# A router's table writes in two runs, and an expert's row transposes one unit earlier

## The chip, the cores and the metric

The kernel runs on one core of a Trainium2 chip. The metric is the device time of one execution in microseconds (us). The core's engines run side by side and wait for each other through semaphores: PE (TensorE, matrix products), DVE (VectorE), ACT (ScalarE), POOL (GpSimd, which here issues the indirect transfers) and SP (SyncE, which issues the plain transfers).

## What is computed

Three layers follow each other: block attention over chunks of 64 tokens, a dense MLP, and a mixture of eight experts of which every token uses two.

```python
x = attention(q, k, v)                        # 2304 tokens x 512
h = x @ w_in;  x = (h * clip(h + 3, 0, 6) / 6) @ w_out          # d_ff 2048
noisy = x @ w_gate + log1p(exp(x @ w_noise)) * noise            # 2304 x 8
top2, top2_w = two largest of noisy per token, softmax of the two
for e in range(8):
    for k in range(2):
        mask = top2[:, k] == e
        out[mask] += top2_w[mask, k, None] * (np.maximum(x[mask] @ w1[e], 0) @ w2[e])
```

## The kernel before

The 2304 tokens are 18 tiles of 128, in five batches of 4, 3, 4, 4 and 3 tiles (`BT`). A batch goes through the dense MLP in 16 units of 128 hidden columns: `mlp_s1` (line 346) makes a unit's hidden values in a PSUM bank, ACT and DVE turn them into the operand `g` (lines 425, 426, 430, 438), and `mlp_o` (line 359) multiplies the unit before into the accumulators. Every product is three passes over high and low parts of the operands, so that a unit of four tiles has 12 matmuls of 512 columns in `mlp_s1` and 12 in `mlp_o`. `regular(b, side, A, B, Z)` writes out batch b's units by hand: the lists A, B, Z and `side` hold what else goes in at each unit. The function `between` fills A, B and Z with the attention of the next batch (scores at line 232, row maximum at 239, subtraction at 249) and with the gate of the batch before. The order of PE, DVE and ACT is the order of the code there; from batch 4 on SP's is, too.

The gate of batch b-1 ends in `gate_ps`. DVE works out, for each token and each of its two experts, a row of a table in DRAM (`slot`, line 623), and POOL writes one entry (token number and weight) for every token by indirect transfers (line 626), one transfer for each tile and each of the two choices: eight for a batch of four tiles. For the first group of four tiles (tokens 0 to 511) this stands at unit 15 of batch 1. Nobody reads the table before batch 4.

Then come the experts as a list of groups: expert 0 in two parts (groups 0 and 1), experts 1 to 6 (groups 2 to 7) and expert 7 in two parts. An expert has eight units u. `exp_h` makes the hidden values of up to 600 rows in two halves of 300 columns, which go to two PSUM banks in turn (line 346, 24 matmuls), ACT and DVE make `g` of each half (lines 716, 717), and `exp_ot` (lines 749, 751, 753) multiplies the unit before. The list `side` says what else goes in at the end of each unit, for the experts that come next:

- `exp_slots_q`: SP loads an expert's slots (line 639) and their transposed copy `tq` (lines 648, 650); `exp_index`: DVE makes row indices `iq` of it (line 658).
- `exp_gather_q`: POOL gathers a tile of 128 rows of x by four indirect transfers (line 663; three for the last tile of 96 rows) into one of three buffers.
- `exp_tr_q`: DVE transposes a gathered tile (line 475), ACT copies it to the high part of the expert's operand (line 675), DVE subtracts for the low part (line 676). The operand alternates between two tiles, `Xa` and `Xe`. The five tiles of an expert are numbered 0 to 4. A gather buffer is free again after line 475.
- `pump`: ACT and DVE split one unit of expert weights (lines 171, 172), and SP loads another (line 165).

In expert 1 (group 2) `exp_tr_q` stood at units 3 to 7 for tiles 0 to 4 of expert 2, whose own units come next:

```python
        elif gi == 2:
            for i in range(nxt_[3]):
                at(side, 3 + i, exp_tr_q, nxt_[0], i)
                if 0 < i < 3:
                    at(side, i, exp_index, nxt_[0], i, (2, nxt_[3])[i - 1])
                if i > 0:
                    at(side, i, exp_gather_q, nxt_[0], i)
```

Of the kernel before, what the change touches and what calls it, by code (L numbers as in the profile page):

```python
# [80 lines left out]
def tile_kernel(ctx, tc, qkv, w1u, w2u, wg, noise, out):  # L81
# [527 lines left out]
        nc.vector.tensor_tensor(offs2, early, base, op=ALU.subtract)  # L609
        nc.vector.scalar_tensor_tensor(offs2, offs2, 0.0, offs, op0=ALU.max, op1=ALU.add)  # L610

    def gate_ps(g):
        t0, nt = GRP[g]
        m12, m = st.pop(("m", g))
        lg = st.pop(("lg", g))
        pos = lg[:, :nt * NE].rearrange("p (t e) -> p t e", t=nt)
        of = offs2 if g == len(GRP) - 1 else offs
        qf = small([P, 5, NE], "qf")[:, :nt]
        nc.vector.tensor_tensor(qf, pos, of[:, None, :].to_broadcast([P, nt, NE]), op=ALU.add)
        nc.vector.tensor_tensor(m12, m12, qf[:, None].to_broadcast([P, 2, nt, NE]), op=ALU.mult)  # L620
        sf = small([P, 2, 5, 1], "sf")[:, :, :nt]
        nc.vector.tensor_reduce(sf, m12, axis=AX.X, op=ALU.add)
        nc.vector.tensor_copy(slot[:, t0:t0 + nt, :], sf.rearrange("p k t o -> p t (k o)"))  # L623
        for t in range(t0, t0 + nt):
            for k in range(2):
                s = nc.gpsimd.indirect_dma_start(  # L626
                    out=table, out_offset=bass.IndirectOffsetOnAxis(ap=slot[:, t, k:k + 1], axis=0),
                    in_=pay[:, t, k, :], in_offset=None)
                for o in st.setdefault("tab_st", []):
                    tc.declare_no_dep(s.ins, o.ins, reason="every slot is given once")  # L630
                st["tab_st"].append(s)
# [372 lines left out]
    def between(b, attn, gates, top, per):  # L1004


        A, B, Z, nt, n0 = {}, {}, {}, BT[b], st.get("tick", 0)
        before = BT[b - 1]

        def s2_(u, k, f, *a):  # L1010
            n = n0 + 3 + k if u == 0 else n0 + 3 + before + (3 + nt) * (u - 1) + 3 + k
            at(ticks, n, f, *a)

        def s1_(u, k, f, *a):
            n = n0 + k if u == 0 else n0 + 3 + before + (3 + nt) * (u - 1) + k
            at(ticks, n, f, *a)


        for i, u in enumerate(attn):
            t = B0[b + 1] + i  # L1020
            if nt > 3:
                s2_(u, nt, att_sc, t, 0, outer)
            else:
                s1_(u, 2, att_sc, t, 0, outer)
            at(B, u, att_mx, t, False)
            at(B, u, att_e, t)
            at(B, u + 1, att_n, t)
            if nt > 3:
                s1_(u + 2, 3, att_pt, t)
                at(A, u + 2, att_at, t, at_[0])  # L1030
                s2_(u + 2, nt, att_xo, t)
                end = (B, u + 2)
            else:
                s2_(u + 2, 1, att_pt, t)
                at(B, u + 2, att_at, t, at_[0])
                s1_(u + 3, 2, att_xo, t)
                end = (Z, u + 3)
            at(*end, att_hi, t)
            at(*end, att_lo, t)
            if t + 2 < NTILE:  # L1040
                at(*end, load_tile, t + 2, bufs[4 + t % 2])
        first = B0[b - 1]
        for u, n in gates:
            ts = list(range(first, first + n))
            first += n
            for i, t in enumerate(ts):
                at(B, u - n - 1 + i, gate_l, t)
                at(B, u - n + i, gate_d, t)
            if nt > 3:
                s2_(u, nt, gate_mm, ts, ENDS[0])  # L1050
                at(B, u, gate_lp, ts)
                s1_(u + 1, 2, gate_rt, ts, ENDS[1])
                s1_(u + 1, 2, gate_rr, ts)
            else:
                p5 = bank("p5", [P, DM], "lg")
                s1_(u + 1, 1, gate_mm, ts, p5)
                at(A, u + 1, gate_lp, ts)
                s1_(u + 2, 1, gate_rt, ts, p5[:, 2 * P:])
                s1_(u + 2, 1, gate_rr, ts)
        for i in range(4):  # L1060
            at(B, top + i // per, gate_top, b - 1, 1)
        pos, pm = ENDS[1] if nt > 3 else bank("p5", [P, DM], "pos"), top + 5 - per
        s2_(pm, 1, gate_pm, b - 1, pos)
        at(B, pm, gate_ps, b - 1)
        return A, B, Z


# [36 lines left out]
    with tc.manual_schedule(engines={nc.tensor.engine, nc.vector.engine, nc.scalar.engine}):  # L1104
        steps(REST)
        prev = [(0, U1 - 1)]
        regular(1, {}, *between(1, (1, 4, 7, 10), ((4, 2), (8, 2)), 12, 2))
        side = {}
        at(side, 10, zero_out)
        regular(2, side, *between(2, (1, 3, 5, 7), ((4, 2), (8, 1)), 10, 2))  # L1110
        side = {}
        for j in range(3):
            at(side, 12 + j, load_raw, U1 + j)
        regular(3, side, *between(3, (1, 3, 5), ((4, 2), (8, 2)), 10, 1))
# [13 lines left out]
    for gi, (key, e, r0, nt, off) in enumerate(groups):  # L1128
# [11 lines left out]
            at(side, 5, exp_gather_q, after[0], 0)  # L1140
        elif gi == 2:
            for i in range(nxt_[3]):
                at(side, 3 + i, exp_tr_q, nxt_[0], i)
                if 0 < i < 3:
                    at(side, i, exp_index, nxt_[0], i, (2, nxt_[3])[i - 1])
                if i > 0:
# [117 lines left out]
```

## Time and profile before

| | |
|---|---|
| runs of the kernel before | 911.08, 912.23, 912.97 us; median 912.23 |
| the profiled execution | 911.34 us |
| its span, first to last instruction | 909.6 us |
| mean granted TensorE clock | 0.996 |
| PE busy | 892.3 us (98% of the span) |
| DVE, ACT, POOL busy | 495.4, 320.6, 230.8 us |
| chain of work that ended last | PE 88%, DVE 5%, DMA 2%, ACT 2%, POOL 1% |

The 1.74 us between the span and the time of the same execution lie outside the first and the last instruction. Of the 17.3 us of the span in which PE is not busy, most is at its start and end. A matmul's end in the profile is modelled, so a stretch of PE is best compared with an equal stretch of the same number and shape of matmuls.

### The profile page before, as it was taken

The page shows a single profiled execution, that of the slowest core. Times are in us where ns is not written, and L with a number is a line of the kernel's source. Part 1 is how long each engine was busy: PE and PEld are TensorE (multiplying, and loading weights), DVE is VectorE, ACT ScalarE, POOL GpSimd, SP SyncE. Part 2 cuts the span into 40 slices and gives each one's busy share as a digit, 9 for nine tenths or more (in the row PEclk, how much of TensorE's full clock was granted, in tenths as well). Part 3 has the DMA queues.
Part 4 walks back from the last instruction along what each step waited for, and adds up shares of the span by engine and source line. Part 5 has one row for each costly group of instructions (what it writes and reads, how often), then busy time and mean ns, then how long its engine had stood idle before and what let it go on. Part 6 is the DMA issues. An engine that isn't in the chain of part 4 may idle for free.

```text
span 909.6 us, 15438 instructions
## 1 busy us (share of the span) xinstructions
PE 892.3 (98%) x6295; PEld 794.0 (87%) x6295; DVE 495.4 (54%) x953; ACT 320.6 (35%) x610; POOL 230.8 (25%) x212
## 2 busy tenths in 40 slices
PE   8999999999999999999999999999999999999995
PEld 5777788887878877888888899999999999999995
DVE  7999955545552553447552544555656555562421
ACT  5555433332332332244551432333333333331110
POOL 0000000030002000023103465455383634606051
PEclk9999999999999999999999999999999999999998
DMA  9745522123228410025541762386786857655462
GB/s 343 251 127 177 172 70 94 36 70 71 71 102 304 129 46 1 1 70 118 157 144 37 171 148 76 92 222 145 200 173 149 188 146 208 151 156 78 111 84 31
DMA packets 68930, 116.39 MB, mean 128 GB/s; under 512 B 17872, under 2 KB 38480, under 8 KB 68848
## 3 DMA queue, kind: packets, MB, share of 16 engines
q1 hardware_dynamic: 57552, 95.33, 35.2%
q0 software_dynamic: 11296, 19.97, 12.4%
q8 instruction: 51, 0.84, 0.4%
q14 instruction: 31, 0.25, 0.1%
HBM read 85.13 MB, written 30.09 MB: 127 GB/s over the span
## 4 chain that ended last, share of the span: by engine, by line
PE 88%; DVE 5%; DMA 2%; ACT 2%; POOL 1%; issue 1%; another core or an unknown queue 1%; SPq 0%; POOLq 0%; ACTq 0%; DVEq 0%
PE bp L346 38%; PE bp L359 21%; PE bp L749 10%; PE bp L753 7%; PE bp L419 4%; PE bp L392 3%; PE pair L314 1%; PE pair L232 1%; POOL table L626 1%; PE pair L293 1%; DMA lead<-in_qkv_dram 1%; DMA table<-pay,slot 1%; DVE u L204 1%; PE bp L690 1%
## 5 line engine op out<-in xcount | busy, mean ns | idle before, releaser
L359 PE MATMUL bp<-w,g 128*128 128x512 f32 (+3 forms) x921 | 230.4, 393 | 0.5 <-ACT g L430 0.4
L359 PEld LDWEIGHTS bp<-w,g 128*128 128x128 f32 (+2 forms) x921 | 166.6, 186 | 35.5 <-DVE g L438 0.9
L346 PE MATMUL bp<-Xa,w 128*128 128x300 f32 (+3 forms) x1152 | 193.7, 319 | 0.5 <-issue 0.3
L346 PEld LDWEIGHTS bp<-Xa,w 128*128 128x128 f32 x1152 | 172.2, 188 | 11.7 <-issue 1.6
L749 PE MATMUL bp<-g,w 128*128 128x352 f32 x576 | 161.4, 323 | 0.0
L753 PE MATMUL bp<-g,w 128*128 128x248 f32 x564 | 155.2, 277 | 0.0
L626 POOL DMA_INDIRECT table<-pay,slot x36 | 36.6, 1015 | 436.7 <-DVE slot L623 427.3
L663 POOL DMA_INDIRECT xrq<-x2d,iq x114 | 117.4, 1030 | 103.7 <-DVE arena L475 62.0
L717 DVE SCALAR_TENSOR_TENSOR g<-bp,g 128x300 fp32r<-128x300 f32 (+2 forms) x127 | 59.2, 470 | 155.1 <-ACT g L716 108.3
L716 ACT ACTIVATE g<-bp 128x300 fp32r<-128x300 f32 (+2 forms) x127 | 53.2, 422 | 224.0 <-PE bp L346 181.2
L749 PEld LDWEIGHTS bp<-g,w 128*128 128x128 f32 x576 | 108.2, 188 | 0.1
L753 PEld LDWEIGHTS bp<-g,w 128*128 128x128 f32 x564 | 106.1, 188 | 0.5
L346 PE MATMUL bp<-Xb,w 128*128 128x384 f32 (+2 forms) x480 | 104.2, 360 | 0.0
L346 PE MATMUL bp<-Xe,w 128*128 128x300 f32 (+1 forms) x672 | 99.8, 303 | 0.0
L346 PEld LDWEIGHTS bp<-Xe,w 128*128 128x128 f32 x672 | 95.5, 188 | 0.8
L346 PEld LDWEIGHTS bp<-Xb,w 128*128 128x128 f32 x480 | 84.7, 188 | 11.3 <-issue 1.1
L172 DVE TENSOR_TENSOR w<-raw,w 128x1024 fp32r<-128x1024 f32 x64 | 78.2, 1222 | 29.2 <-ACT w L171 23.1
L807 POOL DMA_INDIRECT out_dram<-arena,tab x40 | 65.1, 1628 | 104.9 <-ACT arena L787 43.4
L426 DVE SCALAR_TENSOR_TENSOR r<-r,bp 128x384 f32<-128x384 f32 (+1 forms) x64 | 39.7, 620 | 82.5 <-ACT r L425 76.7
L425 ACT ACTIVATE r<-bp,b 128x384 f32<-128x384 f32 (+1 forms) x64 | 40.4, 632 | 106.9 <-PE bp L346 102.6
L171 ACT ACTIVATE w<-raw 128x1024 fp32r<-128x1024 f32 x64 | 67.1, 1049 | 4.7 <-PE bp L359 4.5
L438 DVE TENSOR_TENSOR g<-r,g 128x384 fp32r<-128x384 f32 (+1 forms) x64 | 40.1, 626 | 40.7 <-ACT g L430 39.4
(178 smaller groups left out, 796.9 us busy)
## 6 DMA issues: line engine op xcount, KB each, us to landing
raw<-in_w2u_dram SPq DMA_DIRECT2D x64, 512.0 KB
raw<-in_w1u_dram SPq DMA_DIRECT2D x24, 512.0 KB
arena<-in_qkv_dram SPq DMA_DIRECT2D x14, 768.0 KB
turned<-arena SPq DMA_DIRECT2D x24, 304.0 KB
out_dram<-zero SPq DMA_DIRECT2D x4, 1536.0 KB
yr<-turned SPq DMA_DIRECT2D x6, 1024.0 KB
rawx<-in_w1u_dram SPq DMA_DIRECT2D x8, 512.0 KB
x2d<-x SPq DMA_DIRECT2D x15, 256.0 KB
```

Source lines behind the costliest of these rows:

```text
L171: nc.scalar.activation(w[:, 0], raw, AF.Copy)
L172: nc.vector.tensor_tensor(w[:, 1], raw, w[:, 0].bitcast(F32), op=ALU.subtract)
L346: nc.tensor.matmul(dst, w[:, a, kd * P:(kd + 1) * P], x[:, b, kd, t0:t0 + n], start=(k == 0), stop=(k == 3 * KD - 1))
L359: nc.tensor.matmul(y[:gi.shape[2]], gi[:, a], w[:, b, DM + c:DM + c + y.shape[1]], start=(first and j == 0), stop=(last and j == 2))
L425: nc.scalar.activation(r, st["h", b], AF.Relu, bias=b3)
L626: s = nc.gpsimd.indirect_dma_start(out=table, out_offset=bass.IndirectOffsetOnAxis(ap=slot[:, t, k:k + 1], axis=0), in_=pay[:, t, k, :], i ...
L663: nc.gpsimd.indirect_dma_start(out=xr[:, c * P:(c + 1) * P], out_offset=None, in_=x2q, in_offset=bass.IndirectOffsetOnAxis(ap=st["iq", key ...
L716: nc.scalar.activation(hi[:, t0:t0 + n], h, AF.Relu)
L717: nc.vector.scalar_tensor_tensor(lo[:, t0:t0 + n], h, 0.0, hi[:, t0:t0 + n].bitcast(F32), op0=ALU.max, op1=ALU.subtract)
L749: nc.tensor.matmul(acc[c][:, :BIG], wc, g[a][:, :BIG], start=first, stop=last)
L753: nc.tensor.matmul(small[:, off:off + CAP - BIG], wc, g[a][:, BIG:CAP], start=False, stop=last and off > 0)
L807: s = nc.gpsimd.indirect_dma_start(out=out, out_offset=bass.IndirectOffsetOnAxis(ap=tab[:n, i, 0:1], axis=0), in_=y, in_offset=None, compu ...
```

## The change

`gate_ps` no longer converts all slots of a group and writes all entries. It keeps the slot numbers and calls the new `gate_sc(g, i0, i1)`, which converts those of tiles i0 to i1 and writes their entries. For the first group it is called for tiles 0 and 1 where all four stood, and for tiles 2 and 3 from the side list of batch 2 at unit 1. All other groups are converted and written in one piece as before. In expert 1 the row transposes of expert 2 are written at units 2 to 6 in place of 3 to 7.

```diff
-    def gate_ps(g):
+    def gate_ps(g, n=None):
...
         nc.vector.tensor_reduce(sf, m12, axis=AX.X, op=ALU.add)
-        nc.vector.tensor_copy(slot[:, t0:t0 + nt, :], sf.rearrange("p k t o -> p t (k o)"))
-        for t in range(t0, t0 + nt):
+        st["sf", g] = sf
+        gate_sc(g, 0, n or nt)
+
+    def gate_sc(g, i0, i1):
+        t0 = GRP[g][0]
+        nc.vector.tensor_copy(slot[:, t0 + i0:t0 + i1, :], st["sf", g][:, :, i0:i1].rearrange("p k t o -> p t (k o)"))
+        for t in range(t0 + i0, t0 + i1):
             for k in range(2):
                 s = nc.gpsimd.indirect_dma_start(
...
-        at(B, pm, gate_ps, b - 1)
+        at(B, pm, gate_ps, b - 1, None if b > 1 else 2)
...
         at(side, 10, zero_out)
+        at(side, 1, gate_sc, 0, 2, BT[0])
         regular(2, side, *between(2, (1, 3, 5, 7), ((4, 2), (8, 1)), 10, 2))
...
             for i in range(nxt_[3]):
-                at(side, 3 + i, exp_tr_q, nxt_[0], i)
+                at(side, 2 + i, exp_tr_q, nxt_[0], i)
```

DVE at the seam of batches 1 and 2, before: from the end of `gate_ps` (line 622) to unit 2 of batch 2. `r` and `g` are the MLP's operands, `x` the batch's output, `mx` and `arena` belong to the attention.

```order
L622 TENSOR_REDUCE sf<-m_1985 128x2x4
L623 CAST slot<-sf 128x8
L426 SCALAR_TENSOR_TENSOR r<-r,bp_466 128x512
L438 TENSOR_TENSOR g<-r,g 128x512
L460 TENSOR_SCALAR x_2102<-bp_465 128x512
L426 SCALAR_TENSOR_TENSOR r<-r,bp_467 128x512
L438 TENSOR_TENSOR g<-r,g 128x512
L239 TENSOR_REDUCE mx<-pair_72 128x8
L249 TENSOR_TENSOR arena<-pair_72,mx 128x512
L426 SCALAR_TENSOR_TENSOR r<-r,bp_466 128x512
```

And with the change (the conversion is now line 628):

```order
L622 TENSOR_REDUCE sf<-m_1985 128x2x4
L628 CAST slot<-sf 128x4
L426 SCALAR_TENSOR_TENSOR r<-r,bp_466 128x512
L438 TENSOR_TENSOR g<-r,g 128x512
L460 TENSOR_SCALAR x_2098<-bp_465 128x512
L426 SCALAR_TENSOR_TENSOR r<-r,bp_467 128x512
L438 TENSOR_TENSOR g<-r,g 128x512
L239 TENSOR_REDUCE mx<-pair_72 128x8
L249 TENSOR_TENSOR arena<-pair_72,mx 128x512
L628 CAST slot<-sf 128x4
L426 SCALAR_TENSOR_TENSOR r<-r,bp_466 128x512
```

The conversion of eight columns became two of four, the second seven DVE instructions later, behind the attention's subtraction.

DVE in the last two units of expert 1, before: `g` is the operand of the unit, `arena` and `Xa` the gathered tile of expert 2, `w` a weight unit, and line 706 opens expert 2.

```order
L717 SCALAR_TENSOR_TENSOR g<-bp_466,g 128x300
L717 SCALAR_TENSOR_TENSOR g<-bp_467,g 128x300
L475 STREAM_TRANSPOSE arena<-xrq 128x512
L676 TENSOR_TENSOR Xa<-arena,Xa 128x4x128
L172 TENSOR_TENSOR w<-raw,w 128x1024
L717 SCALAR_TENSOR_TENSOR g<-bp_466,g 128x300
L717 SCALAR_TENSOR_TENSOR g<-bp_467,g 128x300
L475 STREAM_TRANSPOSE arena<-xrq 128x384
L676 TENSOR_TENSOR Xa<-arena,Xa 128x4x96
L706 CAST g<-zeros 128x264
```

And with the change (lines 717, 676, 706 are now 722, 681, 711):

```order
L722 SCALAR_TENSOR_TENSOR g<-bp_466,g 128x300
L722 SCALAR_TENSOR_TENSOR g<-bp_467,g 128x300
L475 STREAM_TRANSPOSE arena<-xrq 128x384
L681 TENSOR_TENSOR Xa<-arena,Xa 128x4x96
L172 TENSOR_TENSOR w<-raw,w 128x1024
L722 SCALAR_TENSOR_TENSOR g<-bp_466,g 128x300
L722 SCALAR_TENSOR_TENSOR g<-bp_467,g 128x300
L711 CAST g<-zeros 128x264
```

The last tile's transpose and subtraction stand ahead of the last unit's two `g` instructions, no longer behind them. The instructions of PE, POOL and SP stand in the same order in both kernels; ACT's copies (line 675) move with the transposes.

## Rows read from the trace of the kernel before

**Rows 1.** The page, part 1: engine, busy us, share, instructions.

```profile
PE 892.3 (98%) x6295; PEld 794.0 (87%) x6295; DVE 495.4 (54%) x953; ACT 320.6 (35%) x610; POOL 230.8 (25%) x212
```

**Rows 2.** Waits of PE, whole span: us in total, times, longest us.

```profile
PE bp L346 <- issue: 0.3, 1, 0.3
PE bp L346 <- DVE Xa L676: 0.2, 1, 0.2
```

**Rows 3.** Timeline of PE, batch 2: start, us, line, tiles, count [idle before <-releaser].

```profile
204.29 0.69 PE L232 MATMUL pair<-arena 64*64 64x64 f32 x32
204.91 1.99 PE L346 MATMUL bp<-Xa,w 128*128 128x512 f32 x7
207.22 1.41 PE L346 MATMUL bp<-Xa,w 128*128 128x512 f32 x5 [0.32 <-issue]
...
218.52 3.03 PE L346 MATMUL bp<-Xa,w 128*128 128x512 f32 x12
```

**Rows 4.** Timeline of POOL: first and last of the first group's eight table writes.

```profile
195.89 1.16 POOL L626 DMA_INDIRECT table<-pay,slot  x1 [193.63 <-DVE slot L623]
...
205.03 0.97 POOL L626 DMA_INDIRECT table<-pay,slot  x1 [0.30 <-issue]
```

**Rows 5.** Timeline of DVE in the same stretch.

```profile
194.79 0.17 DVE L623 CAST slot<-sf 128x8 int32<-128x8 f32 x1
...
207.44 0.69 DVE L239 TENSOR_REDUCE mx<-pair 128x8 f32<-128x512 f32 x1 [2.96 <-remote]
```

**Rows 6.** Timeline of all engines, the row of SP in the same stretch.

```profile
203.69 3.64 SPq L483 DMA_DIRECT2D xq<-x2d  x8
```

**Rows 7.** Windows: stretch, us, PE, PEld, DVE, ACT, POOL busy (count), clock, DMA share, GB/s.

```profile
384.00:396.00 12.00, 12.00 (x59) 10.40 (x57) 3.66 (x6) 3.83 (x7) 7.76 (x8) 1.00 0.20 59
420.00:432.00 12.00, 12.00 (x62) 10.86 (x61) 7.77 (x12) 6.17 (x9) 8.72 (x8) 1.00 0.71 134
...
616.00:628.00 12.00, 12.00 (x90) 12.00 (x89) 6.04 (x9) 4.32 (x7) 9.56 (x9) 1.00 0.84 166
```

**Rows 8.** Timeline of PE: expert 1's last unit and expert 2's first.

```profile
570.28 3.47 PE L346 MATMUL bp<-Xe,w 128*128 128x300 f32 x24
...
576.99 1.98 PE L346 MATMUL bp<-Xa,w 128*128 128x300 f32 x13
579.15 1.78 PE L346 MATMUL bp<-Xa,w 128*128 128x300 f32 x11 [0.19 <-DVE Xa L676]
```

**Rows 9.** Timeline of ACT in expert 1's last unit.

```profile
575.88 0.73 ACT L716 ACTIVATE g<-bp 128x300 fp32r<-128x300 f32 x2 [5.17 <-remote]
```

**Rows 10.** Timeline of DVE at the same seam.

```profile
576.34 0.85 DVE L717 SCALAR_TENSOR_TENSOR g<-bp,g 128x300 fp32r<-128x300 f32 x2 [4.37 <-ACT g L716]
577.10 0.85 DVE L475 STREAM_TRANSPOSE arena<-xrq 128x384 f32<-128x384 f32 x1
578.54 0.56 DVE L676 TENSOR_TENSOR Xa<-arena,Xa 128x384 fp32r<-128x384 f32 x1 [0.59 <-ACT Xa L675]
```

**Rows 11.** Timeline of POOL: first and last of eight gathers for expert 3, and the next.

```profile
564.42 0.95 POOL L663 DMA_INDIRECT xrq<-x2d,iq  x1 [4.81 <-DVE iq L658]
...
573.18 0.95 POOL L663 DMA_INDIRECT xrq<-x2d,iq  x1 [0.30 <-issue]
578.22 0.95 POOL L663 DMA_INDIRECT xrq<-x2d,iq  x1 [4.10 <-DVE arena L475]
```

**Rows 12.** Timeline of DVE: unit 2 of expert 1, up to unit 3's first half.

```profile
541.60 0.22 DVE L658 TENSOR_SCALAR iq<-tq,quarter 128x12 int32<-128x12 int32 x1
542.16 1.23 DVE L172 TENSOR_TENSOR w<-raw,w 128x1024 fp32r<-128x1024 f32 x1 [0.34 <-ACT w L171]
546.17 0.47 DVE L717 SCALAR_TENSOR_TENSOR g<-bp,g 128x300 fp32r<-128x300 f32 x1 [2.78 <-ACT g L716]
```

**Rows 13.** Chain that ended last: start, us, what; one gather's way to its landing.

```profile
441.52 3.94 DMA xr<-x2d,tab
```

## The prediction

> **What bounds the kernel now.** The first thing to read is the share of each engine: PE is busy for 892.3 of 909.6 us, 98%, and the next engine, DVE, for 54% [rows 1]. So a change can only take away places where PE stands still or matmuls that PE need not do. This change does not touch the matmuls. The second view is therefore the list of what PE waited for. Two entries of it lie where the change works, and each occurs once in the whole span: 0.3 us before line 346 with no releaser ("issue"), and 0.2 us before line 346 for the subtraction of line 676 [rows 2]. The third view, the timeline of PE, puts them at 207.22 us (unit 1 of batch 2) and at 579.15 us (expert 2's first unit) [rows 3, 8]. Whatever the change does to other engines, these two places are what it can give back.
>
> The wait that the list shows is less than what PE loses, because the matmuls just ahead of it come late as well. I compare equal blocks. Batch 2's unit 1 has its 12 matmuls of 512 columns from 204.91 to 207.22 + 1.41 = 208.63, 3.72 us; the same 12, also right behind a tile's scores, take 3.03 us at 218.52 [rows 3]. Loss: **0.69 us**. Expert 2's first 24 matmuls run from 576.99 to 579.15 + 1.78 = 580.93, 3.94 us; the 24 of the unit before take 3.47 us [rows 8]. Loss: **0.47 us**.
>
> **Part one, the table writes in two runs.** Before, POOL writes eight transfers in one run, from 195.89 to 205.03 + 0.97 = 206.00, one every (205.03 - 195.89) / 7 = 1.31 us [rows 4]. At the end of that run two things happen together. The scores' matmuls are over at 204.29 + 0.69 = 204.98 [rows 3], yet DVE's row maximum, which waits for nothing but them, starts at 207.44 after an idle time that the profile can only call "remote" [rows 5]: the signal from PE was some 2.5 us late. And PE itself issues its next matmuls 0.69 us late while it waits for nobody. I take both for one cause, a stretch in which signals are held up at the end of a long run of indirect transfers, because the same sign (a late "remote" signal) comes again at 575.88 [rows 9], 1.75 us behind the end of another run of eight, 573.18 + 0.95 = 574.13 [rows 11].
>
> With the change four writes run from 195.89 to about 195.89 + 3 x 1.31 + 0.97 = 200.8, over 3.5 us before the scores start. The second conversion stands on DVE behind the row maximum and the subtraction. If the signal is on time these run from about 205.0 to 206.4, the conversion (at most the 0.17 us of the wide one) to 206.6, and POOL starts 195.89 - 194.79 = 1.1 us after it [rows 4, 5], at about 207.7, and is done at about 212.6. The extra conversion costs nothing: DVE was idle for 2.96 us there [rows 5]; without that cover it would be 0.17 us. No further wait is added on PE, ACT or SP, and nobody reads the table before batch 4. So this part is worth -0.69 us if the run's length is the cause, 0 if it is not, and +0.69 us if the second run brings the same loss to its own end and the first keeps its own. I take -0.69: the loss stands at the end of the run and nowhere near it before. Against it speaks that two other runs of eight writes, from 384 and from 420 us, leave PE at 12.00 of 12.00 us [rows 7].
>
> **Part two, expert 2's transposes one unit earlier.** Before, the last tile's transpose, copy and subtraction come behind both `g` instructions of unit 7. ACT got the hidden values' signal at 575.88, after 5.17 us of idle time [rows 9], so the two `g` instructions ran until 576.34 + 0.85 = 577.19 and the tile from 577.10 to 578.54 + 0.56 = 579.10 [rows 10]; PE, already in expert 2, waited for exactly this. In the changed order the tile is done one unit of 576.99 - 570.28 = 6.7 us earlier [rows 8], ahead of the late signal. The 0.47 us go. What is late next is the PSUM bank: PE starts expert 2 at 576.99, and the first of the two `g` instructions that free its bank ends at about 576.34 + 0.47 = 576.81 (0.47 from rows 12). That leaves 0.18 us of margin.
>
> What the move costs elsewhere: one tile's three steps took 579.10 - 577.10 = 2.0 us for 96 rows [rows 10], so at most 2.7 us for 128. In unit 2, which gets a tile that it did not have, DVE is idle for 0.34 us and 2.78 us, 3.1 us together [rows 12]; it fits, with 0.4 us to spare. Behind it on DVE are queued the index of line 658 and the weight split of line 172, both up to 2.7 us later. The index releases POOL's gather of tile 2: issue at about 545, four transfers 1.25 us apart [rows 11], the last at about 549, landed by 553 if it takes the 3.94 us that a gather on the chain took [rows 13]. It is needed two units behind the index's old place, at 541.6 + 13.4 = 555. The split releases SP's weight load and the slot loads behind it, whose first reader is in unit 5, over 20 us on. Units 3 to 6 trade one tile for the next. Price 0; if the gather's cover went, DVE would wait at the transpose with `g` of the next unit behind it, but by less than the unit's own slack. This part: -0.47 us, bounds -0.47 to what the third rival below costs.
>
> **The sum.** -0.69 - 0.47 = -1.16 us, against the profiled execution's 911.34 us: 910.2. That execution lies 0.89 us below the median of the runs, 912.23; from the median the same difference gives **911.1 us**, -0.13%.
>
> **Rivals.** *First: the stall at 207 is not the run's doing.* SP issued eight transfers from 203.69 to 207.33 [rows 6], just where PE lost its time, and the change leaves these where they are. Together with the two other runs of eight that cost PE nothing [rows 7] this is a serious case. Only part two counts: 912.23 - 0.47 = 911.8. The Trainium skill speaks for this rival: "SBUF — State Buffer", section "Who interferes with whom", states that a DMA never contends with a compute engine and that PE never waits on anyone, and by that rule a run of transfers cannot hold PE, so the sum would be -0.47 rather than -1.16 us. The trace agrees at 384 and 420 us (12.00 of 12.00), not at 207, where PE lost 0.69 us.
>
> *Second: both losses belong to that one execution.* They come from late signals, and three runs of one kernel differ by 1.9 us. Then the change does what it says and nothing comes of it: 912.2.
>
> *Third, slower: the longer gather run.* Tile 4's transpose frees the buffer of expert 3's third tile a unit earlier. Before, POOL stopped for 4.10 us at that point [rows 11]; now it goes on behind the eighth gather, twelve in one run, until about 564.42 + 11 x 1.25 + 0.95 = 579.1. If signals stay late until 1.75 us after the run's end, ACT gets its signal at 580.9 in place of 575.88, the bank is free 0.93 us later, at 581.8, and PE stands from 576.99 on: 4.8 us. With part one's gain the time is 912.23 - 0.69 + 4.8 = 916.3. It decides at 0.18 us: any lateness beyond today's by more than this margin is paid in full. Against it: from 616 to 628 POOL issued nine transfers with hardly a break, 9.56 us busy, and PE was at 12.00 of 12.00 [rows 7].
>
> **How the numbers follow.** Forecast (both go) 0.50; first rival 0.27; second 0.10; third 0.08; unprofiled runs that hold more of such stalls than the profile, and so gain more than 1.16 us, 0.05. A measurement of this kernel tells about 0.2%, 1.8 us, from no change. Faster than that means under 910.4: the last case, and from the forecast and the first rival what the runs' scatter of about 0.9 us puts there, 0.15 together. Slower means over 914.0: the third rival and a remainder of scatter, 0.08. The rest, 0.77, is within 0.2%. The range of 910.0 to 912.9 holds the forecast and the first two rivals with that scatter, and leaves out most of the third.
>
> **What would show it.** Right: 12 matmuls of batch 2's unit 1 in about 3.03 us with no idle time, the row maximum starting near 205 in place of 207.44, two runs of four writes; in expert 2 the first 24 matmuls in about 3.47 us in one piece, the last transpose near 568 to 570. Wrong in part one: a block of 3.7 us again, there or at the second run's end. Wrong in part two: PE waiting at about 577 for line 717's successor, with ACT idle on a late signal behind a gather run of twelve. The prediction as a whole fails if PE's idle time moves by more than these two places, for which I see no cause in the order of instructions.

## The result, and the profile after

The changed kernel takes **920.56 us** (916.16 to 923.01, six runs) beside 912.17 us of the kernel before (911.08 to 912.97, six runs): a ratio of **1.0096**, interval 1.0081 to 1.0110. The forecast was 911.1 us with a range of 910.0 to 912.9; the time lies 7.7 us above its upper end. The profiled execution of after took 922.26 us, 10.92 us more than the one of before.

Page of after, part 1, and below it the waits of PE over the whole span (us in total, times, longest us); the answering rows of before are [rows 1, 2].

```profile
PE 898.8 (98%) x6295; PEld 799.5 (87%) x6295; DVE 494.8 (54%) x954; ACT 321.3 (35%) x610; POOL 231.0 (25%) x212
```

```profile
PE bp L346 <- issue: 1.9, 4, 1.1
...
PE bp L758 <- issue: 1.6, 2, 1.4
...
PE bp L754 <- issue: 1.4, 2, 1.0
```

PE is busy 6.5 us longer with the same 6,295 matmuls, so some of them ran slower, and it stood still for 4.9 us with no releaser, 0.3 us before. The other engines do what they did.

**Part one came out as forecast.** The same seam of batch 2 on PE, DVE and POOL, as in [rows 3 to 5] (columns: start, us, engine, line, operation, tiles, count, [idle before <-releaser]; L631, L628 and L239 of after are L626, L623 and L239 of before):

```profile
204.88 3.03 PE L346 MATMUL bp<-Xa,w 128*128 128x512 f32 x12
```

```profile
205.02 0.69 DVE L239 TENSOR_REDUCE mx<-pair 128x8 f32<-128x512 f32 x1 [0.60 <-PE pair L232]
...
206.35 0.16 DVE L628 CAST slot<-sf 128x4 int32<-128x4 f32 x1
```

```profile
199.89 0.97 POOL L631 DMA_INDIRECT table<-pay,slot  x1 [0.30 <-issue]
206.79 0.97 POOL L631 DMA_INDIRECT table<-pay,slot  x1 [5.93 <-DVE slot L628]
```

The twelve matmuls are in one piece of 3.03 us (3.72 before), and the row maximum starts at 205.02 with PE as its releaser, not at 207.44 as "remote".

**The loss stands in expert 1 and 2.** POOL's gathers, first and last of two runs in which one follows the other after 0.30 us:

```profile
543.52 1.42 POOL L668 DMA_INDIRECT xrq<-x2d,iq  x1 [4.38 <-issue]
...
556.62 0.94 POOL L668 DMA_INDIRECT xrq<-x2d,iq  x1 [0.30 <-issue]
567.85 0.94 POOL L668 DMA_INDIRECT xrq<-x2d,iq  x1 [10.29 <-DVE iq L663]
...
581.94 0.95 POOL L668 DMA_INDIRECT xrq<-x2d,iq  x1 [0.30 <-issue]
```

The first run has eleven gathers (tiles 2 to 4 of expert 2), the second twelve (tiles 0 to 2 of expert 3). PE in the same stretches:

```profile
555.64 0.87 PE L346 MATMUL bp<-Xe,w 128*128 128x300 f32 x4
556.77 0.30 PE L346 MATMUL bp<-Xe,w 128*128 128x300 f32 x1 [0.26 <-issue]
558.17 0.44 PE L346 MATMUL bp<-Xe,w 128*128 128x300 f32 x2 [1.10 <-issue]
...
559.59 4.36 PE L346 MATMUL bp<-Xe,w 128*128 128x300 f32 x16 [0.31 <-issue]
...
567.86 3.48 PE L346 MATMUL bp<-Xe,w 128*128 128x300 f32 x24
...
574.47 3.46 PE L346 MATMUL bp<-Xe,w 128*128 128x300 f32 x24
...
579.91 0.28 PE L758 MATMUL bp<-g,w 128*128 128x248 f32 x1 [0.19 <-issue]
...
582.70 0.37 PE L758 MATMUL bp<-g,w 128*128 128x248 f32 x1 [1.40 <-issue]
...
584.83 0.45 PE L754 MATMUL bp<-g,w 128*128 128x352 f32 x1 [1.03 <-issue]
...
586.29 4.87 PE L346 MATMUL bp<-Xa,w 128*128 128x300 f32 x24
```

and ACT's late signals, as in [rows 9]:

```profile
558.21 0.42 ACT L721 ACTIVATE g<-bp 128x300 fp32r<-128x300 f32 x1 [5.18 <-remote]
584.92 0.73 ACT L721 ACTIVATE g<-bp 128x300 fp32r<-128x300 f32 x2 [10.34 <-remote]
```

Twelve to thirteen us into each run (556.77 against 543.52, 579.91 against 567.85) PE, with no releaser in the profile, begins to bring out its matmuls one by one; the last idle row (559.59, 584.83) is about 2 us behind the end of the run (556.62 + 0.94 = 557.56, 581.94 + 0.95 = 582.89). Then the clock follows. Windows of after (stretch, us, PE, PEld, DVE, ACT, POOL busy, granted clock, DMA share, GB/s):

```profile
540.00:560.00 20.00, 18.07 (x125) 17.22 (x125) 7.75 (x12) 3.91 (x7) 10.99 (x11) 0.97 0.27 65
560.00:580.00 20.00, 19.81 (x124) 19.37 (x123) 8.24 (x13) 5.27 (x9) 9.41 (x10) 0.86 0.34 82
580.00:600.00 20.00, 17.09 (x101) 16.50 (x101) 8.28 (x15) 3.62 (x8) 2.29 (x4) 0.83 0.17 38
558.70:565.50 6.80, 6.32 (x24) 5.93 (x24) 4.79 (x7) 2.31 (x4) 0.00 (x0) 0.50 0.21 55
582.60:589.40 6.80, 5.62 (x22) 5.34 (x22) 1.14 (x3) 0.73 (x2) 0.30 (x1) 0.50 0.05 11
```

From 558.7 to 565.5 and from 582.6 to 589.4 us the granted clock is 0.50, the lower level (1.2 GHz), right behind the stretches in which PE stood idle. The bill: idle 1.93 + 0.19 + 2.91 = 5.03 us in the first three windows; 6.32 + 5.62 = 11.94 us of work at half speed, of which half, 5.97 us, is lost; together **11.0 us**. That is what idle rows and clock show. From start to start the loss is larger:

- The unit from 555.64 to 567.86 us took 12.22 us, the undisturbed one behind it (to 574.47) 6.61: 5.6 us lost.
- The unit from 574.47 to 586.29 us took 11.82 us, in the kernel before 576.99 - 570.28 = 6.71 [rows 8]: 5.1 us lost.
- Expert 2's first 24 matmuls, at half clock, took 4.87 us, those of an undisturbed unit 3.46: 1.4 us lost.

Together 12.1 us. The missing 1.1 us stand in the same stretches, in matmuls that count as busy at full clock. The two executions lie 10.92 us apart, less than that, because the changed kernel was ahead of the other when the first loss began: by part one, and by a wait of 0.37 us for a gather at 445.50 us that of all kept traces only that of the kernel before has.

### The profile page after: what moved, and what is told of

Same layout as the page of the kernel before. It is cut to its first block, busy times and chain, and to the rows that moved or that the text cites. A ratio compares the mean times of both kernels' runs of the same rounds, so it can differ in the third digit from the quotient of the medians.

```text
span 920.4 us, 15437 instructions
## 1 busy us (share of the span) xinstructions
PE 898.8 (98%) x6295; PEld 799.5 (87%) x6295; DVE 494.8 (54%) x954; ACT 321.3 (35%) x610; POOL 231.0 (25%) x212
## 4 chain that ended last, share of the span: by engine, by line
PE 92%; DVE 4%; ACT 1%; issue 1%; DMA 1%; POOL 0%; SPq 0%; POOLq 0%; ACTq 0%; DVEq 0%
PE bp L346 40%; PE bp L359 22%; PE bp L754 10%; PE bp L758 7%; PE bp L419 4%; PE bp L392 3%; PE pair L314 1%; PE pair L232 1%; PE pair L293 1%; DMA lead<-in_qkv_dram 1%; DVE u L204 1%; DVE u L199 1%; PE bp L695 1%; PE bp L731 0%; DVE w L220 0%
## 5 line engine op out<-in xcount | busy, mean ns | idle before, releaser
L754 PE MATMUL bp<-g,w 128*128 128x352 f32 x576 | 163.3, 326 | 1.4 <-issue 1.4
L758 PE MATMUL bp<-g,w 128*128 128x248 f32 x564 | 156.2, 279 | 1.6 <-issue 1.6
L631 POOL DMA_INDIRECT table<-pay,slot x36 | 36.5, 1015 | 438.0 <-DVE slot L628 428.9
L754 PEld LDWEIGHTS bp<-g,w 128*128 128x128 f32 x576 | 109.3, 190 | 2.5 <-issue 2.5
L758 PEld LDWEIGHTS bp<-g,w 128*128 128x128 f32 x564 | 107.2, 190 | 2.1 <-issue 1.6
L346 PE MATMUL bp<-Xe,w 128*128 128x300 f32 (+1 forms) x672 | 102.7, 307 | 1.9 <-issue 1.9
L346 PEld LDWEIGHTS bp<-Xe,w 128*128 128x128 f32 x672 | 97.5, 192 | 3.5 <-issue 2.7
L346 PEld LDWEIGHTS bp<-Xb,w 128*128 128x128 f32 x480 | 84.7, 188 | 11.3 <-issue 1.1
```

The source lines that it names most:

```text
L346: nc.tensor.matmul(dst, w[:, a, kd * P:(kd + 1) * P], x[:, b, kd, t0:t0 + n], start=(k == 0), stop=(k == 3 * KD - 1))
L754: nc.tensor.matmul(acc[c][:, :BIG], wc, g[a][:, :BIG], start=first, stop=last)
L758: nc.tensor.matmul(small[:, off:off + CAP - BIG], wc, g[a][:, BIG:CAP], start=False, stop=last and off > 0)
```

## The experiments

After the first comparison, whose chip is not on record, the kernels ran on six chips, called A to F here. The kernel before, run beside each, took 909.54 us on A, 912.50 on B, 911.21 on C, 909.50 on D, 911.18 on E and 909.48 on F; this difference turned out to be the key. Each ratio is to the kernel before on the same chip.

### Each part alone (chip A)

**Table writes alone**: the changed kernel with the second part put back.

```diff
-                at(side, 2 + i, exp_tr_q, nxt_[0], i)
+                at(side, 3 + i, exp_tr_q, nxt_[0], i)
```

> Only the first group's table writes in two runs; the transposes of expert 2 stand where they did. Run theory (the loss is made by POOL issuing more than eight or nine indirect gathers without a break, which holds up PE's signals and then PE's own issue): this part has no longer run, so 912.2 - 0.7 = 911.5 us, the 12 matmuls of batch 2's unit 1 in about 2.9 us from first start to next block, clock 0.996. Order theory (the loss is made by the moved transposes on DVE and ACT themselves): the same 911.5. Writes theory (the second run of four writes, 8 us later, shifts something that is paid for in expert 1): 918 to 922.

**Transposes alone**: the kernel before with that line of the change and nothing else.

> Only the transposes one unit earlier; the eight table writes stand in one run. Run theory and order theory: both losses of the changed kernel come back and the stall at 207 us too, 920.6 + 0.7 = 921 us (918 to 924), clock 0.989 to 0.994, with two runs of eleven and twelve gathers. Writes theory: 912.2 - 0.5 = 911.7.

**Index by tile**: the changed kernel, with the row numbers of each tile worked out by themselves one unit apart, which was to break the runs of gathers.

```diff
-                if 0 < i < 3:
-                    at(side, i, exp_index, nxt_[0], i, (2, nxt_[3])[i - 1])
                 if i > 0:
+                    at(side, i, exp_index, nxt_[0], i, i + 1)
                     at(side, i, exp_gather_q, nxt_[0], i)
...
-            at(side, 5, exp_index, after[0])
             for i in range(3):
+                at(side, 5 + i, exp_index, after[0], i, (1, 2, CT)[i])
                 at(side, 5 + i, exp_gather_q, after[0], i)
```

> The changed kernel, but in expert 1 DVE computes the row indices of experts 2 and 3 tile by tile, each just ahead of its tile's gathers, where it computed several tiles' indices at once. Transposes stay one unit earlier. POOL then has to wait for DVE between two tiles, and the runs are fours with gaps of 1 us or more. Run theory: both losses go, 912.2 - 0.7 - 0.5 = 911.0 us (910.2 to 912), clock 0.996, ACT's longest wait at the end of expert 1 under 5.2 us. Order theory: no change against the changed kernel, 918 to 923.

**Four more gathers**: the kernel before, with four gathers into a tile that nobody reads behind expert 3's eight.

```diff
+            at(side, 6, exp_more, after[0], 2, 4)
```

> The kernel before, with nothing moved, and four additional gathers (128 rows of 128 bytes each into a scratch tile that nobody reads) written behind the eight gathers for expert 3 in expert 1, so that POOL issues twelve or more without a break from about 564 us on, as in the changed kernel. Run theory: PE loses 5 to 8 us near 577 to 588 us, half-speed clock included, so 917 to 920 us. Order theory: no transposes are moved, so 912.2, within 0.5 us.

Measured: 909.21 us (1.0001, 0.9992 to 1.0010), 909.14 (0.9997, 0.9988 to 1.0006), 909.36 (0.9999, 0.9990 to 1.0008) and 909.42 us (1.0000, 0.9990 to 1.0009). Nothing lost time, which no theory had allowed. The transposes alone made the same two runs of eleven and twelve, the added gathers made one of sixteen (563.60 to 583.29 us), and PE took no notice. The index by tile broke only the eleven here; expert 3's twelve stayed one run (565.50 to 581.24 us). The windows of the transposes alone:

```profile
540.00:560.00 20.00, 20.00 (x147) 20.00 (x146) 10.68 (x17) 6.32 (x11) 11.58 (x11) 1.00 0.34 84
560.00:580.00 20.00, 20.00 (x148) 20.00 (x147) 7.89 (x14) 5.46 (x10) 12.18 (x12) 1.00 0.30 75
580.00:600.00 20.00, 20.00 (x146) 19.91 (x146) 12.86 (x20) 5.81 (x11) 6.61 (x7) 1.00 0.73 192
```

So either both parts are needed together, or the loss depends on the chip.

### The changed kernel again, and its second part alone (chip B)

No edit: the changed kernel, and two of the kernels above once more.

> The changed kernel itself, nothing left out, on the chip of this call beside the kernel before. Condition theory: the late signals behind the long gather runs and PE's stutter there belong to the chip or its condition, not to the program alone. Where the kernel before takes about 909.5 us and PE is at full clock, the changed kernel is within 0.2% of it, every unit of expert 1 and 2 takes 3.30 us per 24 matmuls, and no stretch at half clock follows; where the kernel before takes about 912.2 us, the changed one takes 919 to 922 us. Combination theory: both parts are needed together, so that the changed kernel is 8 to 11 us slower wherever it runs, with both half-clock stretches, even beside a kernel before of 909.5 us.

> The kernel before with the second part of the change alone (expert 2's transposes one unit earlier), which makes the same unbroken runs of eleven and twelve gathers. Condition theory: as the changed kernel of this call, that is within 0.2% of the kernel before where that takes about 909.5 us, and 917 to 922 us where it takes about 912.2. Combination theory: within 0.2% of the kernel before in either case.

> The changed kernel with the row numbers of each tile worked out by themselves, one unit apart, so that POOL's gathers come in fours in place of runs of eleven and twelve. Condition theory with the run's length as the trigger: within 0.2% of the kernel before where that takes about 909.5 us, and about 911 us, 8 to 10 us under the changed kernel, where the kernel before takes about 912.2. If the trigger is the order and not the run's length, it takes the changed kernel's time of this call.

Measured beside 912.50 us: 922.42 us (1.0110, 1.0091 to 1.0129), 924.18 us (1.0136, 1.0118 to 1.0153) and 912.94 us (1.0008, 0.9994 to 1.0023). Combination theory falls: the transposes alone cost as much as the whole change. Windows of the transposes alone on this chip, the same program as in the three rows above:

```profile
540.00:560.00 20.00, 18.18 (x128) 17.64 (x128) 6.63 (x10) 3.91 (x7) 11.12 (x12) 1.00 0.27 68
560.00:580.00 20.00, 19.49 (x138) 18.97 (x138) 9.95 (x15) 6.00 (x11) 8.32 (x9) 1.00 0.29 77
580.00:600.00 20.00, 16.19 (x101) 15.38 (x100) 8.72 (x16) 4.64 (x8) 4.60 (x6) 0.91 0.25 66
```

Up to 560 us POOL does nearly the same on both (11.12 and 11.58 us busy); PE loses 1.82 us there on B and nothing on A. The kernel before is slower on B as well, by 3.0 us. With the index by tile the time is back at that of the kernel before, though some of the loss is left in its trace, 1.17 + 0.43 = 1.6 us of idle time at the second run, which is now eight gathers, a break of 0.89 us and four more:

```profile
560.00:580.00 20.00, 18.83 (x136) 18.66 (x135) 6.50 (x12) 3.80 (x7) 12.64 (x13) 1.00 0.37 95
580.00:600.00 20.00, 19.57 (x138) 19.08 (x138) 12.43 (x20) 6.96 (x12) 5.82 (x7) 1.00 0.61 155
```

### One run at a time, and a longer run without the change (chip C)

**Break the twelve**: index by tile for expert 3 alone. **Break the eleven**: for expert 2 alone. Both are halves of the diff above.

> The changed kernel with the row numbers of expert 3 alone worked out tile by tile, one unit apart: its gathers no longer stand in one run of twelve, while expert 2's run of eleven stays. Theory that each long run costs by itself, on a chip where the kernel before takes about 912 us: the loss at 580 to 590 us goes (7.2 us there in the changed kernel on that chip), the one at 553 to 563 us stays (4.8 us), so about 916 us, with one stretch at half clock at most. Theory that the second loss follows from the first: it does not go, about 922. On a chip where the kernel before takes about 909.5: 909.5 in either case.

> The changed kernel with the row numbers of expert 2 alone worked out tile by tile: no run of eleven, the run of twelve stays. Each run costs by itself, on a chip where the kernel before takes about 912 us: the loss at 553 to 563 us goes, the one at 580 to 590 us stays, about 918 us. The second loss follows from the first: both go, about 912. On a chip where the kernel before takes about 909.5: 909.5 in either case.

**Four more gathers** and **table writes alone**, as on chip A.

> The kernel before with four more gathers of 128 rows of 128 bytes (columns of x that nobody reads, into a tile of their own) behind the eight of expert 3, so that POOL issues twelve to sixteen in one run, while the order of every transpose is as before. Theory of the run's length, on a chip where the kernel before takes about 912 us: 917 to 920 us, with PE standing near 578 to 586 us and a stretch at half clock behind it. Theory of the order (the transposes' new place does it): 912. On a chip where the kernel before takes about 909.5: 909.5 in either case.

> The first part of the change alone (the table writes in two runs) on the chip of this call. If its gain of 0.69 us exists only where signals are late: about 911.5 us where the kernel before takes about 912.2, with 12 matmuls of batch 2's unit 1 in about 3.0 us; no difference where that takes about 909.5.

Measured beside 911.21 us: 913.73 us (1.0034, 1.0022 to 1.0046); 910.81 us (1.0005, 0.9986 to 1.0025); **918.35 us** (1.0071, 1.0046 to 1.0096); 910.22 us (0.9993, 0.9983 to 1.0003).

The four added gathers settle what does it: the order of transposes and index instructions is that of the kernel before, and twelve gathers without a break, on this chip, were enough. POOL, then PE, of that kernel (L671 are the added ones):

```profile
564.97 0.95 POOL L663 DMA_INDIRECT xrq<-x2d,iq  x1 [4.46 <-DVE iq L658]
...
578.75 0.95 POOL L663 DMA_INDIRECT xrq<-x2d,iq  x1 [0.30 <-issue]
```

```profile
576.98 0.33 PE L756 MATMUL bp<-g,w 128*128 128x352 f32 x1 [0.81 <-issue]
...
581.94 5.72 PE L346 MATMUL bp<-Xa,w 128*128 128x300 f32 x20 [0.30 <-issue]
```

The same signs: first idle row 12.0 us after the run's first gather, last one 581.94, 2.2 us behind its end at 579.70; the 20 matmuls of the last row take 5.72 us, at half clock again.

With the twelve broken the eleven still costs, 2.14 us of idle time and no lower clock:

```profile
540.00:560.00 20.00, 17.86 (x127) 17.45 (x126) 7.74 (x12) 3.90 (x7) 11.00 (x11) 1.00 0.26 65
```

With the eleven broken I had expected 918 us if each run costs by itself; two of its nine runs, 913.88 and 917.18 us, went that way, the others did not. The trace names a reason why the whole twelve did little in it: its fourth gather was not like the others.

```profile
569.15 1.84 POOL L668 DMA_INDIRECT xrq<-x2d,iq  x1 [0.30 <-issue]
```

0.9 us longer than the usual 0.95, it stretches the run to 15.6 us. Whether that saved it or the missing first loss did was open here.

### A pause in POOL's issue alone (chips D, E and F)

**Memsets on a tile of their own** between the fours of gathers (seven or two of them), ahead of each run, or between in the eleven alone:

```diff
+    def pause(n):
+        for _ in range(n):
+            nc.gpsimd.memset(work.tile([P, P], F32, tag="rest", bufs=1, name="rest"), 0.0)
```

> The changed kernel with seven memsets of a 128x128 tile that nobody reads on POOL between the fours of gathers of experts 2 and 3 (an estimate of 1.4 to 2 us each, from the 0.2 us that a memset of this size takes); gathers, their order and their index instructions are the changed kernel's. Theory that a run of gathers without a pause does it, on a chip where long runs cost: both losses and both half-clock stretches go, 909.5 to 912 us, within 0.2% of the kernel before. Theory that the place or the order of the gathers does it: 918 to 923 us. On a chip where long runs cost nothing: the time of the kernel before.

> As with seven memsets, but two between the fours (an estimate of 0.4 to 0.6 us). If something builds up while POOL issues one gather per 1.25 us and drains in a pause, so short a pause helps in part: onset later than 11 to 12.7 us after the run's start and 912 to 918 us. If any break of the run is enough: 910 to 912 us. Order theory: 918 to 923 us.

> The control: the same fourteen memsets, all ahead of the first gather of each run, so that the runs of eleven and twelve stay whole. Theory of the missing pause: as the changed kernel, 917 to 923 us on a chip where long runs cost, PE's first gap 10.5 to 13 us after each run's start. If the memsets themselves help: 910 to 912 us.

> Memsets between the fours in expert 2's eleven alone, and all ahead of expert 3's twelve, which stays whole. Each run costs by itself: the loss at 553 to 563 us goes, that at 578 to 590 us stays, 916 to 918 us. The second follows from the first: 910 to 912 us.

These failed as an experiment. The memsets depended on nothing and ran at the start: all 28 of the first kernel began between 2.2 and 9.3 us, and in the other three it was the same. So all four are the changed kernel with its runs whole, on chip D, where the kernel before takes 909.50 us. They took 908.63, 909.10, 909.24 and 908.74 us (0.9992, 0.9993, 1.0000, 0.9992, each within 0.0010). That gives the number still missing: **where the kernel before takes 909.5 us, the whole change costs nothing.**

**Memsets into the gathers' own destination**, which the gathers have to wait for. In this kernel they break the eleven into four and seven and stand ahead of the twelve, which stays whole.

```diff
+        for _ in range(rest):
+            nc.gpsimd.memset(xr, 0.0)
...
-                    at(side, i, exp_gather_q, nxt_[0], i)
+                    at(side, i, exp_gather_q, nxt_[0], i, {3: 3, 4: 3}.get(i, 0))
...
-                at(side, 5 + i, exp_gather_q, after[0], i)
+                at(side, 5 + i, exp_gather_q, after[0], i, {0: 6}.get(i, 0))
```

> The changed kernel with six memsets of the 128x512 destination tiles on POOL (an estimate of 3 us together) behind the first four of expert 2's eleven gathers, and six more ahead of expert 3's twelve, which stay one run. On a chip where long runs cost (the kernel before at 911 to 912.5 us): if a pause alone is enough and each run costs by itself, the units at 553 to 563 us take 3.30 us each, the loss at 578 to 590 us stays, 916 to 919 us; if a pause alone is enough and the second loss follows from the first, neither is there, 910 to 912 us; if order does it, both are there, 918 to 923 us. On a chip where long runs cost nothing (the kernel before at 909.5): 909.5.

Measured on chip E, beside 911.18 us: **915.21 us** (1.0051, 1.0034 to 1.0068). POOL, then PE's windows (PE's first idle row stands at 577.12 us):

```profile
548.16 2.88 POOL L668 MEMSET xrq<- 128x512 f32 x6
551.20 0.95 POOL L670 DMA_INDIRECT xrq<-x2d,iq  x1 [0.16 <-POOL xrq L668]
...
564.07 0.95 POOL L670 DMA_INDIRECT xrq<-x2d,iq  x1 [0.50 <-POOL xrq L668]
...
578.27 0.95 POOL L670 DMA_INDIRECT xrq<-x2d,iq  x1 [0.31 <-issue]
```

```profile
540.00:560.00 20.00, 20.00 (x148) 20.00 (x147) 10.18 (x16) 6.33 (x11) 14.10 (x17) 1.00 0.33 84
560.00:580.00 20.00, 17.79 (x124) 16.80 (x122) 6.53 (x11) 3.80 (x7) 15.08 (x19) 1.00 0.28 72
580.00:600.00 20.00, 19.00 (x126) 18.93 (x127) 10.70 (x18) 5.06 (x9) 3.78 (x4) 0.91 0.49 123
```

One trace holds both cases. The broken run leaves PE at 20.00 of 20.00 us; the whole one costs 2.21 + 1.00 us of idle time and a clock of 0.91 over 20 us, by estimate 0.09 x 20 = 1.8 us more: 5.0 us in the trace, 4.0 us between the medians. So the second loss does not follow from the first, and a pause in POOL's issue was enough to be rid of one, with the order of the gathers and their index instructions unchanged. One thing is taken on trust there: that an unbroken eleven would have cost time on E as it did on B and C. The changed kernel itself did not run on E, and the twelve of the same trace stands in for it. The expected 916 to 919 us were 1 to 4 us too many.

**The same pause in both runs**, and **one memset** in place of six:

> The changed kernel with six memsets (2.9 us together) behind the first four of both runs, so that they are four and seven, four and eight. On a chip where long runs cost (the kernel before at 911 to 912.5 us): both losses go, no stretch at half clock, 909.5 to 911.5 us, at or up to 0.2% under the kernel before. If anything but the unbroken run costs too: 913 us or more. On a chip where long runs cost nothing (the kernel before at 909.5): 909.

> The same with a single memset (0.5 us) at the same two places. On a chip where long runs cost: if any break starts the count of the run anew, as with six memsets, 909.5 to 911.5 us; if what builds up drains only as long as POOL pauses, most of the loss stays, 914 to 921 us, with the first gap later than 12.7 us after the run's start. On a chip where long runs cost nothing: 909.

Measured on chip F, beside 909.48 us: 908.85 us (0.9996, 0.9986 to 1.0006) and 909.34 us (1.0001, 0.9991 to 1.0011). By the time of the kernel before F is a chip like A and D, on which long runs cost nothing in any case, so how long a pause must be (on B a break of 0.89 us behind eight gathers left 1.6 us of idle time), and what the changed kernel takes with both runs broken by memsets on a chip like B, stays open. The index by tile is the only cure of both that was measured there, and it brings the time back to that of the kernel before, not below it: no version was found that beats both kernels.

## Why the prediction was wrong, point by point

*What bounds the kernel.* Right in that only what PE lost moved the time, though half of it was matmuls at half clock and not standing still. But the list of PE's waits was read as a list of what the change could give back; what it could take was not looked for with the same care.

*Part one.* Right in its place and its size, -0.69 us in the trace (3.03 us for 3.72). On chip C, alone, it measured 0.99 us less than the kernel before, with an interval that includes zero. The first rival (the stall at 207 is not the run's doing) falls: SP's eight transfers still run there in after, for 4.41 us from 203.47, and PE takes no notice; on B, with the eight writes in one run, the transposes alone show an idle row of 0.69 us at 207.33; on C the writes in two runs show twelve matmuls in 3.03 us. On A the run of eight costs nothing either, so that there is nothing to win there. Why two other runs of eight writes cost nothing in any trace [rows 7] stays open. The Trainium skill's rule that I weighed ("SBUF — State Buffer", section "Who interferes with whom": a DMA never contends with a compute engine, PE waits for nobody) fits the traces of A and D and not those of B, C, E and the first comparison, where PE stands for whole microseconds with no releaser while POOL does nothing but start transfers; the section speaks of ports of the memory, and the traces do not say where PE is held.

*Part two.* The transposes did move, and the wait at the seam went: expert 2's first 24 matmuls are one row without idle time (586.29 us), a gain that the losses around it hide. On A there was nothing to win here either: with the transposes in their old place the 24 take 3.46 us in one piece (table writes alone, 575.29 us). The step that failed is the "Price 0" for the move. I followed the index instruction to the four gathers of one tile ("the last at about 549") and stopped. The next two tiles stand behind it on POOL. Their row numbers come from the same index instruction, and their buffers are freed by the transposes of tiles 0 and 1, which now stand a unit earlier, at

```profile
540.17 1.08 DVE L475 STREAM_TRANSPOSE arena<-xrq 128x512 f32<-128x512 f32 x1
...
546.78 1.08 DVE L475 STREAM_TRANSPOSE arena<-xrq 128x512 f32<-128x512 f32 x1
```

in place of 548.21 and 554.81 us. So in place of the two breaks of before (start, us, and in brackets the idle time of POOL)

```profile
549.56 0.95 POOL L663 DMA_INDIRECT xrq<-x2d,iq  x1 [1.60 <-DVE arena L475]
...
556.16 0.95 POOL L663 DMA_INDIRECT xrq<-x2d,iq  x1 [1.91 <-DVE arena L475]
```

there is none from 543.52 to 557.56. This eleven, which cost 5.6 us, is in no part of the prediction. Each queue that a released instruction stands in has to be followed until it next stops.

*The third rival* named the twelve, its cause and its direction, and was near in its end (579.1 forecast, 582.89 measured, the run having begun 3.4 us later behind the first loss). Its signal to ACT came 2.0 us behind the run's end (584.92 against 582.89), where it had 1.75, and this is also the sign that the prediction had named for being wrong in part two. It failed in three points:
- Its path. The 4.8 us were to be paid by PE waiting for the PSUM bank behind ACT's late signal. That bank was free at about 584.92 + 0.93 = 585.85 us (the 0.93 as in the prediction), and PE opened expert 2 at 586.29; but PE had been held before that, from 579.91 on, in matmuls for which the profile shows no releaser (L758, L754), as it had been at 207 us [rows 3]. The two delays lie over each other, so that the 5.1 us lost up to expert 2 are near the 4.8 by luck. ACT's signal was late before PE first stood: in the undisturbed unit it came 1.9 us after the block's start (569.78 against 567.86), so here it was due at about 576.4. How the late signal and the held PE hang together these traces do not say.
- The clock was not in it. By the rows, 5.97 of the 11.0 us for both runs come from the half-clock stretches behind the idle ones.
- Its chance, 0.08. The forecast rested on signals being held up at the end of a run of indirect transfers, and the third rival on the same cause with a longer run. Where the first holds, the second is likely, and the margin of 0.18 us was named as the point where it decides. The two should not have been 0.50 and 0.08.

The evidence that I set against it was true and is not explained away by the result. The stretch from 616 to 628 us [rows 7] is part of a run of seventeen transfers of the kernel before with no break over 0.31 us (POOL, then the window with PE at 28.00 of 28.00 us):

```profile
604.64 1.62 POOL L807 DMA_INDIRECT out_dram<-arena,tab  x1 [3.52 <-ACT arena L787]
...
617.68 1.60 POOL L807 DMA_INDIRECT out_dram<-arena,tab  x1 [0.30 <-DVE Xe L676]
...
628.92 0.95 POOL L663 DMA_INDIRECT xrq<-x2d,iq  x1 [0.30 <-issue]
```

```profile
604.00:632.00 28.00, 28.00 (x206) 28.00 (x205) 14.75 (x23) 10.24 (x17) 20.36 (x17) 1.00 0.71 150
```

The same mixed run comes in the later experts, in the changed kernel too (seventeen from 615.25 to 641.93 us), and PE never stands. Five of the seventeen are stores of results (L807), 1.9 us apart, and at most eight gathers follow each other. So it is not the length without a break alone that costs. Whether it is the rate, the kind of transfer or the place in the program, no run separates.

*The second rival* (the losses belong to one execution) was nearer than I thought in kind, and wrong in what varies: not the execution but the chip, or its condition.

## What to carry to other kernels

Before an instruction is released earlier, write down how many transfers its queue will now issue without a stop, and give that length a price of its own: on the chips where it counted, eight gathers or table writes in a row cost nothing to 0.7 us, eleven 2.5 to 5.6 us, twelve 4 to 7 us, except in the kernel with the eleven broken, where twelve with one transfer 0.9 us longer cost nothing in seven of nine runs. With slower stores among them, seventeen cost nothing. One pause of 3 us inside the eleven left PE without a loss there and needed no other order. If two branches of a forecast rest on one cause, give them one chance; and time a change on more than one chip before believing either sign.

## What the runs showed of the hardware

- **The same program loses 12 us on one chip and nothing on another.** Transposes alone: 909.14 us on A (before 909.54), 924.18 us on B (before 912.50). Long runs cost on B, C and E and, by its times and trace, on the chip of the first comparison; they cost nothing on A and D, and F was not asked. The time of the kernel before, 911 to 912.5 us or 909.5, told which kind it was. What differs in the chips, or whether it is a condition that comes and goes, these runs cannot say.
- **Where it costs, it has a fixed shape.** The runs that cost are gathers or table writes alone. PE's first idle row stands 11.3 us (207.22 against 195.89, [rows 3, 4]) to 13.3 us (556.77 against 543.52) after the first transfer of an unbroken run, at one transfer per 1.25 to 1.31 us, and the last one about 2 us after the run's end (2.0, 1.9, 2.2 us above). A run of eight is over after 10 us and so just touches it. This looks like something that fills up while POOL issues without a pause and drains when it stops; the pause on chip E fits that, and the seventeen with slower stores, which cost nothing, fit it only if it drains at their rate too; but no run shows what it is, and it is a reading, not a finding.
- **A few microseconds of stutter can cost as many again in the clock.** After PE's idle rows, none longer than 1.4 us, the granted clock was at 0.50 for 6.8 us, twice in after; with the twelve broken on chip C PE was idle for 2.14 us and the clock stayed at 1.00.
